# Gated recurrence and max-out MLP in one kernel: first loads in another order, unit 1's steps up to its masks ahead of MoE 0

## The chip, the cores and the metric

The kernel runs on one NeuronCore of a Trainium2 chip. The metric is the device time of one execution in microseconds; lower is better. The core has a matrix engine (TensorE, PE), a vector engine (VectorE, DVE), a scalar engine (ScalarE, ACT), a general engine (GpSimd, POOL) and a queue that here issues all DMAs (SyncE, SP). Each takes its instructions strictly in order, and they wait for each other through semaphores.

## The reference, cut to what matters

```python
batch, n_heads, seq, head_dim = (4, 8, 768, 48)      # q, k, v, alpha
for t in range(S):
    state = alpha[:, :, t, :, None] * state + np.einsum('bhd,bhe->bhde', k[:, :, t], v[:, :, t])
    y[:, :, t] = np.einsum('bhd,bhde->bhe', q[:, :, t], state)
x = y.transpose(0, 2, 1, 3).reshape(B * S, H * D)     # 3072 x 384
h1 = x @ w1                                           # w1, w2: 384 x 1024
h2 = x @ w2
out = np.maximum(h1, h2) @ w_out                      # w_out: 1024 x 384
```

A gated linear recurrence over 768 steps, then an MLP with a max of two branches. Everything comes and goes in float32.

## The kernel before, in words

The recurrence is done in chunks of 128 steps. A **unit** is two chunks of one batch entry with all 8 heads (256 tokens); there are 12 units, u = 0 to 11, and unit u continues the state of unit u - 4. For a unit the attention part is, in this order: ln (ScalarE: logarithm of alpha), sums (TensorE: running sums of it), exps (ScalarE: expm, expp for both chunks, then expd), kmul (GpSimd) and qmul (VectorE), which scale k and q, turn (TensorE transposes, copied by VectorE into qk), vcast (GpSimd and ScalarE: v to 16 bit), pmm and pmask (TensorE products of q and k; VectorE masks them into pt), kvmm, kvsum and state (the chunk's contribution to the state; state makes sb on GpSimd), ystate and yin (TensorE: the outputs y, copied to xn by ScalarE), xturn (transposes y to xt).

The MLP of a unit ("MoE u") is four steps hid (TensorE, then a relu that makes gT) and two steps outp. The max is rewritten: max(h1, h2) = relu(h1 - h2) + h2. So hid uses w12 = w1 - w2 (wsub, VectorE, one quarter of the columns at a time), and h2 @ w_out becomes x @ w2o with w2o = w2 @ w_out. That product is made in the kernel once: w2h is w2 in 16 bit, wturn transposes it into w2T, wcast makes w_out 16 bit (half by ScalarE, half by GpSimd), wmul multiplies into three accumulators wq, wout copies them to w2o.

All steps are written out by hand and every engine gets its instructions in the order of the program text (`tc.manual_schedule()`, L465). So a step that stands earlier in the text stands earlier in the queue of each engine it uses, SyncE's too. The loads of units 0 and 1 and of the weights stand first (L113 to L122); load(2) to load(5) stand in the hand-written start, load(u + 4) at the head of iteration u of the loop from L569. Loads rotate through four buffers (ldp). The loop runs attention of unit u beside the MLP of unit u - 1 and prepares unit u + 1; iteration u begins with kvmm(u, 0).

Two places matter for what follows. The result tile of a unit has two buffers, and both copies of a unit come before its one DMA to memory, which SyncE issues in its order (after load(u + 5)):

```python
X["outs"] = mp.tile([128, 2, DM], FP32, tag="outs", bufs=2, name="outs")   # L412
nc.scalar.copy(out=X["outs"][:, n, :], in_=op)                             # L420
nc.sync.dma_start(out=dst, in_=X["outs"])                                  # L426
```

And the accumulator banks are shared by tags: "m" (two banks) serves hid, outp, wturn and the warm-up matmuls (dummies, which keep TensorE busy and have no use for the result), "pp" (two) serves pmm, "g" (four) the rest of the attention part.

Of the kernel before, what the change touches and what calls it, by code (L numbers as in the profile page):

```python
# [15 lines left out]
def kernel(  # L16
# [73 lines left out]
    def load_a(u):  # L90
        load_fat(u, "af", alpha)
# [8 lines left out]
    def load(u):  # L100
        load_a(u)
        if u in PAIRED:
            load_fat(u, "kf", k)
            load_fat(u, "qf", q)
        else:
            load_kq(u, 0)
            load_kq(u, 1)
        load_v(u)
# [4 lines left out]
    load(0)  # L113
    for ds in range(ND):
        nc.sync.dma_start(out=w2f[:, ds], in_=moe_w2[ds * 128 : (ds + 1) * 128])
    for n in range(2):
        f = slice(n * NF // 2, (n + 1) * NF // 2)
        nc.sync.dma_start(out=wof[:, f], in_=moe_w_out.rearrange("(s p) d -> p s d", p=128)[:, f])
    for n in range(4):
        f = slice(n * DFF // 4, (n + 1) * DFF // 4)  # L120
        nc.sync.dma_start(out=w1f[:, :, f], in_=moe_w1.rearrange("(s p) f -> p s f", p=128)[:, :, f])  # L121
    load(1)  # L122

    wz = constp.tile([128, 512], FP16)
    nc.vector.memset(wz, 0.0)
# [57 lines left out]
    def new(tag, shape, dtype, bufs, name):  # L183
        return psp.tile(shape, dtype, tag=tag, bufs=bufs, name=name)


    def ln(u):
        X = st[u]
        X["lg"] = LG[u % NB]
        nc.scalar.activation(  # L190
            out=X["lg"][:, :, :, 0:D], in_=X["af"].rearrange("p h j d -> p j h d"), func=ACTF.Ln
        )
# [15 lines left out]
    def sums(u):  # L208
        X = st[u]
        lg = X["lg"]  # L210
        cs = [new("g", [128, 512], FP32, 4, "cs") for _ in range(2)]
        X["csv"] = csv = [x[:, 0 : H * D].rearrange("p (h d) -> p h d", h=H) for x in cs]
        X["dps"] = dps = cs[0][:, H * D : H * D + 4 * HP].rearrange("p (j b n) -> p j b n", j=HP, b=2)
        for hp in range(HP):
            for j in range(2):
                nc.tensor.matmul(
                    dps[:, hp], lhsT=pair(lg[:, j], hp), rhs=halves, start=(j == 0), stop=(j == 1)
                )
        for j in range(2):
            for i in range(2):  # L220
                if u in PAIRED:
                    m, x = mf[:, j, i].rearrange("p c t -> p (c t)"), lg[:, j, :, 0:D]
                else:
                    r = slice(64 * i, 64 * i + 64)
                    m, x = mc[r, j], lg[r, j, :, 0:D]
                nc.tensor.matmul(csv[i], lhsT=m, rhs=x, start=(j == 0), stop=(j == 1))  # L226
        X["qn"], X["kn"], X["Em"] = [], [], []
        for cc in range(2):
            X["qn"].append(QN[(2 * u + cc) % (2 * NB)])
            X["kn"].append(KN[(2 * u + cc) % (2 * NB)])  # L230

    def expm(u, cc):
        X = st[u]
        Em = gp.tile([128, H, D], FP32, tag="Em", name="Em")
        X["Em"].append(Em)
        nc.scalar.activation(out=Em, in_=X["csv"][cc], func=ACTF.Exp, scale=-1.0)  # L236

    def expp(u, cc):

        X = st[u]  # L240
        nc.scalar.activation(out=X["csv"][cc], in_=X["csv"][cc], func=ACTF.Exp)  # L241
# [106 lines left out]
    def ystate(u):  # L348
        X = st[u]
        X["ya"] = ya = [new("g", [128, 2, HP, D], FP32, 4, "ya") for _ in range(2)]  # L350
        X["begun"] = begun = set()
        for cc in range(2):
            if ("sb", cc) not in X:
                continue
            for j in range(HP):
                for a in range(2):
                    r = slice(64 * a, 64 * a + D)
                    nc.tensor.matmul(
                        ya[a][:, cc, j, :], lhsT=X["qk"][r, cc, j, :], rhs=X["sb", cc][r, j, :],
                        start=a not in begun, stop=False,  # L360
                    )
                    begun.add(a)

    def yin(u):
        X = st[u]
        ya, begun = X["ya"], X["begun"]
        for cc in range(2):
            for a in range(2):
                for j in range(HP):
                    nc.tensor.matmul(  # L370
                        ya[a][:, cc, j, :], lhsT=X["pt", cc][:, a, j, :], rhs=X["v16"][:, cc, 2 * j + a, :],
                        start=a not in begun, stop=(cc == 1 and j == HP - 1),
                    )
                    begun.add(a)
        X["xn"] = xn = gp.tile([128, 2, HP, 2, D], FP16, tag="xn", name="xn")
        for a in range(2):
            nc.scalar.copy(out=xn[:, :, :, a, :], in_=ya[a])  # L377

    def xturn(u):
        X = st[u]  # L380
        xp = new("g", [128, ND, 2, C], FP16, 4, "xp")
        for cc in range(2):
            xf = X["xn"][:, cc].rearrange("p j a d -> p (j a d)")
            for ds in range(ND):
                o = xp[:, ds].rearrange("p j (c t) -> p c j t", c=2)[:, cc]
                nc.tensor.transpose(o, xf[:, ds * 128 : (ds + 1) * 128], ident)  # L386
        X["xt"] = mp.tile([128, ND, 2, C], FP16, tag="xt", bufs=3, name="xt")
        nc.vector.tensor_copy(out=X["xt"], in_=xp)  # L388

    def hid(u, f2, on_act=None):  # L390
        X = st[u]
        if f2 == 0:
            X["gT"] = mp.tile([128, NF, 2 * C], FP16, tag="gT", name="gT")
        gT = X["gT"]
        hp = new("m", [128, 2, 2 * C], FP32, 2, "hp")
        for n in range(2):
            f = 2 * f2 + n
            for ds in range(ND):
                nc.tensor.matmul(  # L399
                    hp[:, n, :], lhsT=w12[:, ds, f * 128 : (f + 1) * 128],  # L400
                    rhs=X["xt"][:, ds].rearrange("p n t -> p (n t)"), start=(ds == 0), stop=(ds == ND - 1),
                )
        if f2 != 3 if on_act is None else on_act:
            nc.scalar.activation(out=gT[:, 2 * f2 : 2 * f2 + 2, :], in_=hp, func=ACTF.Relu)  # L404
        else:
            nc.vector.tensor_relu(out=gT[:, 2 * f2 : 2 * f2 + 2, :], in_=hp)  # L406
# [21 lines left out]
    def wturn(ds):  # L428
        wt = new("m", [128, NF, 128], FP16, 2, "wt")
        for f in range(NF):  # L430
            nc.tensor.transpose(wt[:, f, :], w2h[:, ds, f * 128 : (f + 1) * 128], ident)
        nc.vector.tensor_copy(out=w2T[:, :, ds * 128 : (ds + 1) * 128], in_=wt)

    wqs = []

    def wmul(n):

        if n == 0:
            wqs.extend([new("pp", [128, DM], FP32, 2, "wq") for _ in range(2)] + [new("g", [128, DM], FP32, 4, "wq")])
        for ds in range(ND):  # L440
            for f in range(4 * n, 4 * n + 4):
                nc.tensor.matmul(  # L442
                    wqs[ds], lhsT=w2T[:, f, ds * 128 : (ds + 1) * 128], rhs=wo16[:, f, :],
                    start=(f == 0), stop=(f == NF - 1),
                )
# [5 lines left out]
    def wcast(n):  # L451
        nc.scalar.copy(out=wo16[:, 4 * n : 4 * n + 2], in_=wof[:, 4 * n : 4 * n + 2])
        nc.gpsimd.tensor_copy(out=wo16[:, 4 * n + 2 : 4 * n + 4], in_=wof[:, 4 * n + 2 : 4 * n + 4])

    def wsub(n):
        f = slice(n * DFF // 4, (n + 1) * DFF // 4)
        nc.vector.tensor_sub(out=w12[:, :, f], in0=w1f[:, :, f], in1=w2f[:, :, f])

    def dummies(n):

        warm = new("m", [128, 512], FP32, 2, "warm")
        for _ in range(n):
            nc.tensor.matmul(warm, lhsT=wz[:, 0:128], rhs=wz, start=True, stop=True)  # L463
# [29 lines left out]
    pmm(0, 1)  # L493
    pmask(0, 1)
    kvsum(0, 1)
    ystate(0)
    dummies(2)
    wturn(1)
    yin(0)
    wturn(2)  # L500
    wcast(0)
    dummies(2)
    xturn(0)
    ln(1)
    dummies(4)
    wmul(0)
    wcast(1)
    wsub(0)
    wsub(1)
    wsub(2)  # L510
    wsub(3)
    wmul(1)
    sums(1)
    wout()

    load(3)
    hid(0, 0, False)
    expm(1, 0)
    expp(1, 0)
    hid(0, 1, True)  # L520
    kmul(1, 0)
    qmul(1, 0)
    expm(1, 1)
    expp(1, 1)
    hid(0, 2, False)
    expd(1)
    kmul(1, 1)
    qmul(1, 1)
    vcast(1)
    hid(0, 3, True)  # L530
    load(4)
    turn(1, 0)
    turn(1, 1)
    outp(0, 0)
    kvmm(1, 0)
    pmm(1, 0)
    kvmm(1, 1)
    kvsum(1, 0)
    state(1, 1)
    pmask(1, 0)  # L540
    kvsum(1, 1)
    ln(2)
    dummies(3)
    pmm(1, 1)
    pmask(1, 1)
    ystate(1)
    outp(0, 1)
    yin(1)
    sums(2)
    exps(2)  # L550
    dummies(3)
    xturn(1)
    for cc in range(2):
        kmul(2, cc)
    state(2, 0)
    vcast(2)
    for cc in range(2):
        qmul(2, cc)
    dummies(2)
    hid(1, 0)  # L560
    hid(1, 1)
    turn(2, 0)
# [84 lines left out]
```

## Time and profile before

| what | value |
|---|---|
| median of 7 runs | 156.89 us (156.48 to 157.63) |
| the profiled execution | 156.89 us, span 155.2 us |
| mean granted TensorE clock | 0.978 |
| TensorE busy | 140.3 us, 90% |
| VectorE, ScalarE, GpSimd busy | 93.9, 91.5, 56.4 us |
| moved by DMA | 28.58 MB, mean 184 GB/s |
| share of the end's chain on TensorE | 68% |

The span runs from the first to the last instruction. All times given as moments are counted from its start. In the lists of a profile a line gives the start, the duration, the engine, the line of the kernel, the operation with out<-in and shapes, how many were merged (x), and in brackets how long the engine stood idle before and what ended that. A busy TensorE need not be at its peak: matmuls are pipelined, and the granted clock says how fast it may run.

### The profile page before, as it was taken

The page shows a single profiled execution, that of the slowest core. Times are in us where ns is not written, and L with a number is a line of the kernel's source. Part 1 is how long each engine was busy: PE and PEld are TensorE (multiplying, and loading weights), DVE is VectorE, ACT ScalarE, POOL GpSimd, SP SyncE. Part 2 cuts the span into 40 slices and gives each one's busy share as a digit, 9 for nine tenths or more (in the row PEclk, how much of TensorE's full clock was granted, in tenths as well). Part 3 has the DMA queues.
Part 4 walks back from the last instruction along what each step waited for, and adds up shares of the span by engine and source line. Part 5 has one row for each costly group of instructions (what it writes and reads, how often), then busy time and mean ns, then how long its engine had stood idle before and what let it go on. Part 6 is the DMA issues. An engine that isn't in the chain of part 4 may idle for free.

```text
span 155.2 us, 4245 instructions
## 1 busy us (share of the span) xinstructions
PE 140.3 (90%) x1683; PEld 101.3 (65%) x1683; DVE 93.9 (60%) x191; ACT 91.5 (59%) x188; POOL 56.4 (36%) x111
## 2 busy tenths in 40 slices
PE   6956982999999898999999999999999999999991
PEld 2334741575677586777787777877778778767760
DVE  5068682075548878776687784957757577664110
ACT  3565404483293778576696584966938669444421
POOL 7481300065071626319046172371632806410000
PEclk9999598699999999999999999999999999999999
DMA  4999999989797999969989799997989002020202
GB/s 115 265 384 376 359 299 224 207 154 246 132 252 121 275 200 200 183 123 315 160 250 194 138 298 143 257 188 148 300 135 301 8 6 95 4 101 4 94 7 101
DMA packets 76339, 28.58 MB, mean 184 GB/s; under 512 B 71712, under 2 KB 74528, under 8 KB 76320
## 3 DMA queue, kind: packets, MB, share of 16 engines
q1 hardware_dynamic: 76320, 28.32, 79.3%
q8 instruction: 13, 0.21, 0.6%
q14 instruction: 6, 0.05, 0.1%
HBM read 23.59 MB, written 4.72 MB: 182 GB/s over the span
## 4 chain that ended last, share of the span: by engine, by line
PE 68%; SPq 8%; DMA 7%; DVE 6%; ACT 5%; issue 4%; POOL 1%; ACTq 0%; DVEq 0%
PE op L417 20%; PE hp L399 16%; PE op L415 8%; DMA af<-in_alpha_dram 7%; PE tp L285 6%; SPq L121 4%; PE pp L334 3%; PE cs L226 3%; DVE pt L340 3%; PE wq L442 2%; SPq L75 2%; PE xp L386 2%; PE ya L370 2%; PE kv L307 2%; ACT cs L241 2%
## 5 line engine op out<-in xcount | busy, mean ns | idle before, releaser
L274 POOL TENSOR_TENSOR kn<-kf,Em 128x384 f16<-128x384 f32 x24 | 23.5, 998 | 35.3 <-ACT Em L236 33.8
L399 PE MATMUL hp<-xt,w 128*128 128x256 f16 x288 | 35.7, 273 | 0.4 <-DVE xt L388 0.2
L417 PE MATMUL op<-wo,gT 128*128 128x384 f16 x192 | 35.1, 326 | 0.0
L340 DVE TENSOR_TENSOR pt<-pp,um 128x512 f16<-128x512 f32 x48 | 30.9, 686 | 3.1 <-PE pp L334 2.4
L420 ACT COPY outs<-op 128x384 f32<-128x384 f32 x24 | 11.5, 479 | 35.4 <-PE op L417 35.4
L399 PEld LDWEIGHTS <-w 128*128 128x128 f16 x288 | 26.7, 98 | 5.0 <-issue 1.0
L417 PEld LDWEIGHTS <-gT 128*128 128x128 f16 x192 | 18.8, 98 | 12.4
L266 POOL TENSOR_TENSOR sb<-tm,dd 128x192 f16<-128x192 f32 x20 | 10.1, 506 | 42.2 <-DVE tm L320 23.1
L404 ACT ACTIVATE gT<-hp 128x512 f16<-128x512 f32 x35 | 20.8, 598 | 4.8 <-PE hp L399 3.8
L292 DVE COPY qk<-tp 128x1024 f16<-128x1024 f16 x20 | 13.7, 687 | 11.7 <-PE tp L285 11.7
L406 DVE TENSOR_SCALAR gT<-hp 128x512 f16<-128x512 f32 x13 | 9.0, 692 | 16.1 <-PE hp L399 16.1
L320 DVE TENSOR_TENSOR tm<-kv,sb 64x192 f32<-64x192 f32 x32 | 11.3, 352 | 8.7 <-PE kv L307 8.4
L415 PE MATMUL op<-w2o,xt 128*128 128x384 f16 x72 | 15.6, 325 | 0.5
L278 DVE TENSOR_TENSOR qn<-qf,cs 128x384 f16<-128x384 f32 x24 | 12.3, 547 | 5.3 <-ACT de L246 5.0
L190 ACT ACTIVATE lg<-af 128x768 f16<-128x768 f32 x12 | 10.1, 843 | 8.1 <-DMA af<-in_alpha_dram 7.8
L377 ACT CAST xn<-ya 128x384 f16<-128x384 f32 x24 | 10.4, 491 | 4.8 <-PE ya L370 4.4
L204 ACT CAST v<-vf 64x384 f16<-64x384 f32 x24 | 12.2, 510 | 1.4 <-DMA vf<-in_v_dram 0.9
L463 PE MATMUL warm<-wz 128*128 128x512 f16 x35 | 11.9, 462 | 1.3 <-DVE halves L146 1.3
L236 ACT ACTIVATE Em<-cs 128x384 f32<-128x384 f32 x24 | 11.8, 490 | 1.9 <-PE cs L226 1.4
L202 POOL CAST v<-vf 64x384 f16<-64x384 f32 x24 | 12.0, 501 | 0.8
L334 PE MATMUL pp<-qk 48*128 48x128 f16 x192 | 10.4, 217 | 1.6 <-DVE pt L340 1.2
L241 ACT ACTIVATE cs<-cs 128x384 f32<-128x384 f32 x24 | 11.8, 492 | 0.0
(60 smaller groups left out, 166.9 us busy)
## 6 DMA issues: line engine op xcount, KB each, us to landing
af<-in_alpha_dram SPq DMA_DIRECT2D x12, 384.0 KB, 5.7
vf<-in_v_dram SPq DMA_DIRECT2D x12, 384.0 KB, 4.9
out_dram<-outs SPq DMA_DIRECT2D x11, 384.0 KB, 4.3
kf<-in_k_dram SPq DMA_DIRECT2D x40, 96.0 KB, 4.4
qf<-in_q_dram SPq DMA_DIRECT2D x40, 96.0 KB, 4.0
w2f<-in_moe_w_dram SPq DMA_DIRECT2D x3, 512.0 KB, 5.9
wof<-in_moe_w_out_dram SPq DMA_DIRECT2D x2, 768.0 KB, 9.0
w1f<-in_moe_w_dram SPq DMA_DIRECT2D x4, 384.0 KB, 10.9
```

The costliest lines, as they stand in the source:

```text
L202: nc.gpsimd.tensor_copy(out=o, in_=i)
L204: nc.scalar.copy(out=o, in_=i)
L241: nc.scalar.activation(out=X["csv"][cc], in_=X["csv"][cc], func=ACTF.Exp)
L274: nc.gpsimd.tensor_mul(out=X["kn"][cc][:, :, 0:D], in0=part(u, "kf", cc), in1=X["Em"][cc])
L278: nc.vector.tensor_mul(out=X["qn"][cc][:, :, 0:D], in0=part(u, "qf", cc), in1=X["csv"][cc])
L292: nc.vector.tensor_copy(out=X["qk"][:, cc], in_=tp.rearrange("p n h t -> p (n h) t"))
L334: nc.tensor.matmul(pa[a][:, j, :], lhsT=qk[r, 1, j, :], rhs=qk[r, 0, j, :], start=True, stop=True)
L340: nc.vector.tensor_mul(out=pt[:, a], in0=X["pa", cc][a], in1=um.unsqueeze(1).to_broadcast([128, HP, C]))
L399: nc.tensor.matmul(hp[:, n, :], lhsT=w12[:, ds, f * 128 : (f + 1) * 128], rhs=X["xt"][:, ds].rearrange("p n t -> p (n t)"), start=(ds == 0 ...
L404: nc.scalar.activation(out=gT[:, 2 * f2 : 2 * f2 + 2, :], in_=hp, func=ACTF.Relu)
L415: nc.tensor.matmul(op, lhsT=X["xt"][:, ds, n, :], rhs=w2o[:, ds, :], start=(ds == 0), stop=False)
L417: nc.tensor.matmul(op, lhsT=X["gT"][:, f, n * C : (n + 1) * C], rhs=wo16[:, f, :], start=False, stop=(f == NF - 1))
```

## The change

The three big loads alpha, k and q of unit 1 move from behind all the weights to between w2 and w_out; w1 becomes the last of the weights, and v of unit 1 stays behind it. In the hand-written start the steps of unit 1 from ln to pmask move from beside and behind MoE 0 to ahead of it, and are interleaved with the making of w2o. Two of the three wq accumulators take banks of tag "m" instead of "pp". The four relus of MoE 0 all go to ScalarE. wsub is spread between pmask and the hid steps. Warm-up matmuls are regrouped (33 instead of 35). The loop from L569 and the computation are the same. New line numbers are 3 higher behind the loads.

```diff
     load(0)
     for ds in range(ND):
         nc.sync.dma_start(out=w2f[:, ds], in_=moe_w2[ds * 128 : (ds + 1) * 128])
+    load_a(1)
+    load_fat(1, "kf", k)
+    load_fat(1, "qf", q)
     for n in range(2):
         f = slice(n * NF // 2, (n + 1) * NF // 2)
         nc.sync.dma_start(out=wof[:, f], in_=moe_w_out.rearrange("(s p) d -> p s d", p=128)[:, f])
     for n in range(4):
         f = slice(n * DFF // 4, (n + 1) * DFF // 4)
         nc.sync.dma_start(out=w1f[:, :, f], in_=moe_w1.rearrange("(s p) f -> p s f", p=128)[:, :, f])
-    load(1)
+    load_v(1)
...
         if n == 0:
-            wqs.extend([new("pp", [128, DM], FP32, 2, "wq") for _ in range(2)] + [new("g", [128, DM], FP32, 4, "wq")])
+            wqs.extend([new("m", [128, DM], FP32, 2, "wq") for _ in range(2)] + [new("g", [128, DM], FP32, 4, "wq")])
...
     pmm(0, 1)
     pmask(0, 1)
     kvsum(0, 1)
+    dummies(2)
+    wturn(1)
+    ln(1)
+    dummies(2)
+    sums(1)
     ystate(0)
-    dummies(2)
-    wturn(1)
+    exps(1)
     yin(0)
+    kmul(1, 0)
+    kmul(1, 1)
     wturn(2)
+    dummies(2)
+    qmul(1, 0)
+    qmul(1, 1)
+    xturn(0)
+    turn(1, 0)
+    dummies(2)
+    turn(1, 1)
     wcast(0)
-    dummies(2)
-    xturn(0)
-    ln(1)
-    dummies(4)
+    pmm(1, 0)
+    pmask(1, 0)
     wmul(0)
     wcast(1)
     wsub(0)
+    pmm(1, 1)
+    pmask(1, 1)
+    wmul(1)
+    wout()
+
+    load(3)
+    hid(0, 0, True)
     wsub(1)
+    hid(0, 1, True)
     wsub(2)
+    dummies(2)
+    hid(0, 2, True)
     wsub(3)
-    wmul(1)
-    sums(1)
-    wout()
-
-    load(3)
-    hid(0, 0, False)
-    expm(1, 0)
-    expp(1, 0)
-    hid(0, 1, True)
-    kmul(1, 0)
-    qmul(1, 0)
-    expm(1, 1)
-    expp(1, 1)
-    hid(0, 2, False)
-    expd(1)
-    kmul(1, 1)
-    qmul(1, 1)
+    dummies(2)
     vcast(1)
     hid(0, 3, True)
     load(4)
-    turn(1, 0)
-    turn(1, 1)
     outp(0, 0)
     kvmm(1, 0)
-    pmm(1, 0)
     kvmm(1, 1)
     kvsum(1, 0)
     state(1, 1)
-    pmask(1, 0)
     kvsum(1, 1)
     ln(2)
-    dummies(3)
-    pmm(1, 1)
-    pmask(1, 1)
+    outp(0, 1)
     ystate(1)
-    outp(0, 1)
     yin(1)
     sums(2)
+    dummies(2)
+    xturn(1)
     exps(2)
-    dummies(3)
-    xturn(1)
     for cc in range(2):
         kmul(2, cc)
...
         qmul(2, cc)
-    dummies(2)
     hid(1, 0)
     hid(1, 1)
```

More of the change, by code (lines that the diff above doesn't have):

```diff
@@ L495 @@
     kvsum(0, 1)
-    ystate(0)
     dummies(2)
     wturn(1)
+    ln(1)
+    dummies(2)
+    sums(1)
+    ystate(0)
+    exps(1)
     yin(0)
+    kmul(1, 0)
+    kmul(1, 1)
     wturn(2)
+    dummies(2)
[5 more added lines that the diff above has]
+    turn(1, 1)
     wcast(0)
-    dummies(2)
-    xturn(0)
-    ln(1)
-    dummies(4)
+    pmm(1, 0)
+    pmask(1, 0)
     wmul(0)
@@ L508 @@
     wsub(0)
-    wsub(1)
-    wsub(2)
-    wsub(3)
+    pmm(1, 1)
+    pmask(1, 1)
     wmul(1)
-    sums(1)
     wout()
     load(3)
-    hid(0, 0, False)
-    expm(1, 0)
-    expp(1, 0)
+    hid(0, 0, True)
+    wsub(1)
     hid(0, 1, True)
-    kmul(1, 0)
-    qmul(1, 0)
-    expm(1, 1)
-    expp(1, 1)
-    hid(0, 2, False)
-    expd(1)
-    kmul(1, 1)
-    qmul(1, 1)
+    wsub(2)
+    dummies(2)
+    hid(0, 2, True)
+    wsub(3)
+    dummies(2)
     vcast(1)
```

## The prediction

> **What bounds the kernel now.** The page first: it cuts the 155.2 us span into forty slices of 3.88 us.
>
> ```profile
> PE   6956982999999898999999999999999999999991
> PEclk9999598699999999999999999999999999999999
> DMA  4999999989797999969989799997989002020202
> ```
>
> TensorE is full from about 31 us on; its holes and its only low-clock slices lie in the first 30 us, where the change works. But the transfers too are busy until 120 us, and that decides this forecast. The chain of waits, in order of time, says what fills the start:
>
> ```profile
> 13.88 10.66 DMA af<-in_alpha_dram
> 24.55 0.84 ACT lg L190
> 25.40 0.73 ACT wo L452
> 26.17 3.76 PE wq L442 x12
> ```
>
> ScalarE waits for unit 1's alpha, issued behind all weights and landing at 13.88 + 10.66 = 24.5; the second wcast stands behind ln(1) on its queue though its data had landed at 17.1 (issue 7.29 + 9.8), and wmul(1) waits for that. Next, equal stretches with TensorE's granted clock (columns: stretch; busy us of PE, PEld, DVE, ACT, POOL; clock; DMA share; GB/s):
>
> ```profile
> 12.50:15.90 3.40, 1.86 (x40) 1.31 (x38) 3.35 (x8) 1.21 (x2) 1.11 (x2) 1.00 1.06 375
> 15.90:19.30 3.40, 3.40 (x37) 2.67 (x35) 2.01 (x5) 1.59 (x3) 0.99 (x2) 0.50 1.08 356
> 22.70:26.10 3.40, 0.00 (x0) 0.00 (x0) 1.37 (x2) 1.55 (x2) 0.00 (x0) 1.00 0.94 217
> 26.10:29.50 3.40, 3.33 (x11) 1.62 (x11) 0.00 (x0) 0.97 (x3) 0.00 (x0) 0.51 1.06 248
> ```
>
> A stretch of 3.4 us that is empty, or only 55% busy (1.86 of 3.40), is followed by 3.4 us at half clock: the same twelve wq matmuls took 2.11 us at 20.50 and 3.76 at 26.17, so one such stretch costs up to 1.65 us.
>
> Last, the place that I expect to matter afterwards: the output of unit 1 on SyncE, then ScalarE and TensorE in iteration u = 4 (start, duration).
>
> ```profile
> 67.51 0.52 SPq L426 DMA_DIRECT2D out_dram<-outs  x1
> ```
> ```profile
> out_dram<-outs SPq DMA_DIRECT2D x1, 384.0 KB, 5.2
> ```
> ```profile
> 73.72 0.48 ACT L420 COPY outs<-op 128x384 f32<-128x384 f32 x1 [1.08 <-PE op L417]
> 74.23 1.04 ACT L204 CAST v<-vf 64x384 f16<-64x384 f32 x2
> ```
> ```profile
> 75.24 1.46 PE L417 MATMUL op<-wo,gT 128*128 128x384 f16 x8
> 76.54 0.33 PE L307 MATMUL kv<-v,kn 128*128 128x96 f16 x4
> ```
>
> The tile outs has two buffers, so the copy at 73.72 (unit 3) may not start before the output of unit 1 has landed, at 67.51 + 5.2 = 72.7. It had 1.0 us to spare. That output was ready at 55.4; it went out at 67.5 because SyncE issues in order and had loads 5 and 6 before it.
>
> **The start, part by part.** Up to pmm(0,1) at 13.9 nothing changes. *Loads.* The third part of w2 lands at 6.4 + 6.5 = 12.9 as before. Loads of 384 KB land 1.3 to 1.5 apart (25.9, 27.4, 28.7 for unit 1), so alpha, k, q of unit 1 land at 14.4, 15.8, 17.3 instead of 24.5, 25.9, 27.4. The halves of w_out (2.1 apart before) then land at 19.4 and 21.5 instead of 15.0 and 17.1; w1's quarters (6.0 for four) at 23.0, 24.5, 26.0, 27.5 instead of 19.6 to 23.1; v of unit 1 at 28.7, as before: the bytes ahead of it are the same. On SyncE's queue three issues (1.3 to 1.5 each when not blocked) pass ahead of six weight issues; the engines hold 4 to 6 us of issued work all the time, which covers that.
>
> *Unit 1 ahead of MoE 0.* ScalarE: ln(1) 14.4 to 15.2. TensorE: dummies and wturn(1) to 15.4, sums(1) (1.0) to 16.4, ystate(0), yin(0), wturn(2), dummies to 18.4 (0.3, 0.55, 0.6, 0.45), all at full clock, since the hole 13.9 to 15.35 is now filled. ScalarE: exps(1) take 1.75 (6.40 to 8.15 for unit 0), so xn(0), queued behind them, ends at 19.05 (before 18.5): xturn(0) is 0.4 later, of no account. VectorE: qmuls to 19.8, xt, two qk copies (0.7 each) to 21.8; GpSimd: kmuls 17.0 to 19.0, wcast 20.3. TensorE: turns to 21.0, pmm(1,0) 22.3, wmul(0) (2.1) 24.4, pmm(1,1) 24.8, wmul(1) 26.9. VectorE alternates pmask(1,0) to 23.5, wsub(0) 25.0, pmask(1,1) 26.3 and the other wsubs (0.95 each) to 29.1, each after its quarter of w1. Since wq now sits in the m banks, hid(0,0) also waits for wout's first copy (26.0): hidden. hid(0,0) starts at 26.9; before, 30.6.
>
> *From there to hid(1,0).* Before 13.7 (30.62 to 44.34). After: four hid (0.75) with four dummies 3.9, two outp 3.6, kvmm 0.6, ystate and yin 0.85, sums(2) 0.75, dummies 0.45, xturn and its copy 1.15: 11.3. The turns, the pmm behind pmask and four of eight dummies left this stretch. The relus moved from VectorE (0.69) to ScalarE (0.60) hide behind the hids; vcast(1) (v at 28.7) is done at 31.4, needed at 32.6. Thus hid(1,0) is at 38.2 instead of 44.3: **6.1 us earlier**. If w1 is 1 us late, wsub(3) has 0.9 to spare; if the clock drops once, 1.65 goes; I keep 4 to 6.5.
>
> **What is late next.** Loads of the later units keep pace with a shift of 6: the tightest, v of unit 3, lands at 45.2 and is needed at 53.8 - 6 = 47.8. The outputs do not. Every wait that SyncE has on an engine up to 67.5 is satisfied long before (load 6's buffers are free from 46 us), the DMA share of its stretches from 30 to 66 averages 1.0, so SyncE's stream is set by the transfers alone and doesn't get faster when TensorE does. The output of unit 1 still lands at about 72.7, while the outs copy of unit 3 would be due at 73.7 - 6.1 = 67.6. ScalarE stands for 5 us. Queued behind it: vcast(5), outs(3,1), ln(6), then gT. TensorE can end outp(3,1) at 70.6, then kvmm(5,0) needs v's first cast: 72.7 + 0.48 + 0.04 + 0.51 + 0.06 = 73.8. Before it started at 76.5, so **2.7 us of the 6.1 remain**, and TensorE stood for 3.2 us. The next output (77.24 + 4.8 = 82.0) meets a copy due at 83.8 - 2.7 = 81.1: 0.9 late, but kvmm has 1.6 to spare there. After that the spare grows.
>
> **The clock.** A hole of 3.2 us in stretches of 3.4 leaves one of them less busy than the 55% of the row above, so I expect half clock after it: bounds 0 and 1.65. Part of the low stretch can fall in the wait itself; I take 1.3, near the row. Net 2.7 - 1.3 = 1.4. The Trainium skill (TensorE: Matmul & The Clock Gate, Part 1) states that the clock falls after at least one idle window of about 3.4 us; by that rule a 3.2 us hole is spared and the time would be 154.2. The row at 12.5, throttled after a hole of only 1.5 us within it, speaks against that, and here the row decides.
>
> **Sum.** The profiled execution took 156.89 (span 155.2 and 1.69 around it), equal to the median 156.89: 156.9 - 1.4 = **155.5 us**.
>
> **Rivals.** (1) *The wait without the clock*: full clock through the hole; 156.9 - 2.7 = 154.2. For: the phase of the stretches is not the program's. Against: both rows above. (2) *The start's gain kept*: outputs leave earlier, nothing waits; 156.9 - 6.1 = 150.8. Against: SyncE's order and a full DMA row. (3) *Slower: the stream of loads starts later.* Before, kf and qf of unit 1 blocked SyncE for 4.62 and 2.69 us against 1.33 for vf, up to 4.7 too long, and the DMA share fell to 0.55 at 25.2 to 26.0. If the same blocking now stands ahead of w_out and w1 and the engines run dry, all later loads and the output of unit 1 slip by d; kvmm(5,0) is at 73.8 + d plus 1.3 for the clock, so it is slower once d passes 1.4; at d = 2.5 158.0. Against: the same bytes, and 4 to 6 us of issued work as cover. (4) *The start gains nearly nothing*, because w_out and w1 come 4.4 us later and hold wmul and hid(0,0): 156.5 to 157.2. Against: wmul(1) is at 24.8 by its TensorE queue, w_out at 21.5.
>
> **How the numbers follow.** Half a per cent, 0.8 us, is about what a measurement of this kernel can tell from no change. Main case 50% (154.9 to 156.3; 0.44 of it faster, 0.06 same); rival 1 17%; rival 2 7%; rival 3 16% (0.13 slower, 0.03 same); rival 4 10% (0.08 same, 0.02 slower). Faster 0.68, same 0.17, slower 0.15. The range, 153.8 to 157.4, leaves out rival 2 and the larger half of rival 3.
>
> **What would show it.** Right: lg of unit 1 near 14.4; no empty stretch at 22.7; hid(1,0) near 38; the output of unit 1 issued at 67 to 68; an idle time of ScalarE of 4 to 5 us before outs(3,0), ended by that DMA; a TensorE hole near 71 to 74, a low clock after it, and from there a lead of 1 to 3 us that stays. Wrong: that output issued well before 66 or after 69, or the lead gone before iteration u = 2.

## The result, and the profile after

The changed kernel took 158.24 us (median of 14 runs, 157.64 to 159.07) against 156.79 (35 runs) on the same chip: ratio 1.0079, 95% interval 1.0054 to 1.0103. It is slower by 0.8%, where 0.9% faster was forecast. (Three of the ten executions of one later run, the one with TensorE kept busy, fell into a slower state, and its ratio leaves them out.) Its profiled execution took 158.15 us, span 156.4. Lines of the changed kernel are three higher from load_v on: the copy into outs is L423, the output DMA L429.

The same three rows of its page (slices of 3.91 us):

```profile
PE   6859879998789899991699999999999999999991
PEclk9999999999999999998579999999999999999998
DMA  4999999879799998979989799898998402020202
```

The low clock of the first 30 us is gone; one empty slice (the digit 1, at 70 to 74 us) and one low-clock stretch behind it are new. The start did what was forecast. Timeline, ScalarE's lg of unit 1 and TensorE's hid(0,0) and hid(1,0) (start, duration, and in brackets the idle time before and what ended it):

```profile
14.49 0.84 ACT L193 ACTIVATE lg<-af 128x768 f16<-128x768 f32 x1 [0.46 <-DMA af<-in_alpha_dram]
```
```profile
26.15 1.67 PE L402 MATMUL hp<-xt,w 128*128 128x256 f16 x12
37.58 1.47 PE L402 MATMUL hp<-xt,w 128*128 128x256 f16 x12 [0.65 <-DVE xt L391]
```

The stretches that were shown of before, in the same view and then the hole, in the steps of 3.41 us in which the clock changed:

```profile
12.50:15.90 3.40, 3.27 (x52) 2.12 (x50) 3.36 (x7) 2.06 (x3) 0.51 (x1) 1.00 1.27 267
15.90:19.30 3.40, 2.73 (x46) 1.75 (x44) 2.75 (x7) 2.51 (x7) 1.96 (x2) 1.00 1.11 344
22.70:26.10 3.40, 3.40 (x28) 1.93 (x27) 2.68 (x5) 1.72 (x3) 0.83 (x1) 1.00 1.12 335
26.10:29.50 3.40, 3.32 (x24) 2.07 (x22) 2.57 (x3) 2.09 (x5) 0.52 (x2) 1.00 1.13 222
```
```profile
70.06:73.47 3.41, 0.83 (x6) 0.29 (x3) 0.05 (x1) 0.00 (x0) 0.00 (x0) 1.00 0.82 240
73.47:76.88 3.41, 1.02 (x13) 0.68 (x14) 0.40 (x2) 2.01 (x5) 0.00 (x0) 0.50 1.14 221
76.88:80.30 3.42, 3.42 (x28) 2.45 (x28) 2.21 (x5) 1.67 (x3) 0.51 (x1) 0.50 0.73 132
```

The first stretch of the hole has 0.83 us of TensorE work, the second 1.02; two stretches, not one, run at half clock, the second and the one behind it. The chain of waits names the cause:

```profile
69.47 5.25 DMA out_dram<-outs
74.71 0.02 issue
74.73 0.02 ACTq L423
74.75 0.04 issue
74.79 0.48 ACT outs L423
75.27 0.02 issue
75.29 0.52 ACT v L207
75.81 0.04 issue
75.86 0.50 PE kv L310 x4
```

The output of unit 1 goes out at 69.47, not 67.51, and lands at 74.7, not 72.7. The copy outs(3,0) waits for it with 8 us of ScalarE idle in front, v of unit 5 is cast behind that copy, and TensorE stands until 75.86. From the timeline of TensorE, kvmm(5,0), the hid behind it, and kvmm(6,0); then, of the kernel before, hid(1,0) and kvmm(6,0):

```profile
75.86 0.50 PE L310 MATMUL kv<-v,kn 128*128 128x96 f16 x4 [4.97 <-ACT v L207]
77.13 2.76 PE L402 MATMUL hp<-xt,w 128*128 128x256 f16 x12
87.82 0.33 PE L310 MATMUL kv<-v,kn 128*128 128x96 f16 x4
```
```profile
44.34 1.47 PE L399 MATMUL hp<-xt,w 128*128 128x256 f16 x12 [0.22 <-DVE xt L388]
86.59 0.33 PE L307 MATMUL kv<-v,kn 128*128 128x96 f16 x4
```

Of a lead of 6.76 us at hid(1,0) (44.34 to 37.58), 0.68 is left at kvmm(5,0) (76.54 to 75.86). From there to kvmm(6,0) it takes 11.96; before it took 10.05 (76.54 to 86.59). The 1.91 us between are the half clock: twelve hid matmuls in 2.76 instead of 1.47. Thus 156.89 - 0.68 + 1.91 = 158.12, against 158.15 measured.

### The profile page after: what moved, and what is told of

The parts are those of the page before. It is cut to its first block, busy times and chain, and to the rows that moved or that the text cites. A ratio compares the mean times of both kernels' runs of the same rounds, so it can differ in the third digit from the quotient of the medians.

```text
span 156.4 us, 4240 instructions
## 1 busy us (share of the span) xinstructions
PE 139.5 (89%) x1681; PEld 99.7 (64%) x1681; DVE 92.4 (59%) x189; ACT 92.7 (59%) x190; POOL 56.5 (36%) x111
## 4 chain that ended last, share of the span: by engine, by line
PE 54%; SPq 22%; DMA 7%; ACT 6%; DVE 4%; issue 4%; ACTq 0%; DVEq 0%
PE op L420 17%; PE hp L402 13%; SPq L75 9%; SPq L85 7%; PE op L418 7%; PE tp L288 5%; DMA vf<-in_v_dram 4%; DMA out_dram<-outs 3%; PE pp L337 3%; SPq L124 3%; PE cs L229 2%; DVE pt L343 2%; PE kv L310 2%; ACT cs L244 2%; PE xp L389 2%
## 5 line engine op out<-in xcount | busy, mean ns | idle before, releaser
L402 PE MATMUL hp<-xt,w 128*128 128x256 f16 x288 | 37.4, 279 | 1.6 <-ACT gT L407 0.8
L423 ACT COPY outs<-op 128x384 f32<-128x384 f32 x24 | 11.5, 479 | 38.0 <-PE op L420 30.1
L402 PEld LDWEIGHTS <-w 128*128 128x128 f16 x288 | 27.2, 100 | 7.5 <-issue 2.6
L407 ACT ACTIVATE gT<-hp 128x512 f16<-128x512 f32 x37 | 22.0, 598 | 6.9 <-PE hp L402 6.0
L409 DVE TENSOR_SCALAR gT<-hp 128x512 f16<-128x512 f32 x11 | 7.6, 692 | 8.0 <-PE hp L402 8.0
L466 PE MATMUL warm<-wz 128*128 128x512 f16 x33 | 11.0, 449 | 1.3 <-DVE halves L149 1.3
```

Source lines behind the costliest of these rows:

```text
L402: nc.tensor.matmul(hp[:, n, :], lhsT=w12[:, ds, f * 128 : (f + 1) * 128], rhs=X["xt"][:, ds].rearrange("p n t -> p (n t)"), start=(ds == 0 ...
```

## The experiments

Theory 1: the start's gain is eaten by the wait of outs(3,0) for the output of unit 1, which lands later than before, and by the clock behind the hole. Rivals: the gain is lost to later loads, or to another queue. Landings below are the issue's start plus the time to landing; "lead" is against the kernel before.

**A third buffer of outs, in the changed kernel and in the kernel before.**

```diff
-X["outs"] = mp.tile([128, 2, DM], FP32, tag="outs", bufs=2, name="outs")
+X["outs"] = mp.tile([128, 2, DM], FP32, tag="outs", bufs=3, name="outs")
```

> The changed kernel with three buffers for the result tile instead of two, nothing else. Theory 1 (the lead of 6.8 us at hid(1,0) is lost at one place, where the copy of unit 3's result waits for the output of unit 1, and by the low clock after it): the copy of unit 3 needs no buffer that is still going out, the copy of unit 4 (due at 83.8 - 6.8 = 77) needs the output of unit 1 (landed at 74.7), so no wait; the hole at 71 to 76 and the low clock are gone; 150 to 151 us. Theory 2 (the slipped stream of loads itself is the bound, the output is only the first to show it): the wait turns up at a load, vf or kf of unit 5 or 6, and the time stays at 156 to 158 us.

> The kernel before with three buffers for the result tile. Control for the first run: theory 1 has the copy of unit 3 with 1.0 us to spare in the kernel before, so a third buffer gives nothing: 156.5 to 157.1. If the kernel before also waited for its outputs somewhere, it would be faster by over 0.8 us.

Measured: the changed kernel 150.26 us (ratio to before 0.9572, 0.9517 to 0.9627); the kernel before 156.47 (0.9966, 0.9909 to 1.0024, no difference that can be told). ScalarE's copies outs(3,0) and outs(4,0) of the first:

```profile
67.07 0.48 ACT L423 COPY outs<-op 128x384 f32<-128x384 f32 x1 [1.08 <-PE op L420]
77.12 0.48 ACT L423 COPY outs<-op 128x384 f32<-128x384 f32 x1 [1.08 <-PE op L420]
```

Both wait for TensorE alone. The output of unit 1 landed at 74.0 here, almost as late, and it did not matter. kvmm(5,0) stood 6.65 us ahead (76.54 to 69.89):

```profile
69.89 0.33 PE L310 MATMUL kv<-v,kn 128*128 128x96 f16 x4
```

The start's gain arrives whole, and 156.89 - 6.65 = 150.24. The wait, not the loads, held it, and the same buffer is worth nothing where nothing waits.

**The output ahead of load 6, two buffers.** In the changed kernel load(u+4) moves to the end of iteration u.

```diff
-        if u + 4 < NU:
-            load(u + 4)
...
+        if u + 4 < NU:
+            load(u + 4)
```

> The changed kernel with load(u+4) moved from the start to the end of iteration u, so that SyncE issues the output of unit 1 behind load 5 and before load 6; outs keeps its two buffers. Theory 1 (the wait is made by SyncE's order, the output queued behind a load that is not urgent): the output of unit 1 lands some 5 us earlier, at 68 to 70, when the copy outs(3,0) is due at about 67.5; the wait shrinks to 0 to 2 us, no low clock follows, 150 to 152. Theory 2 (the transfers themselves are the limit: what goes out first delays the loads behind it by as much): v or k of unit 5 or 6 comes late instead, and the time stays above 155.

Measured: 150.55 us (0.9613, 0.9551 to 0.9675). SyncE's issue of the output of unit 1, and outs(3,0):

```profile
60.12 0.52 SPq L429 DMA_DIRECT2D out_dram<-outs  x1
```
```profile
67.10 0.48 ACT L423 COPY outs<-op 128x384 f32<-128x384 f32 x1 [1.08 <-PE op L420]
```

Theory 1 again, by the other end: the output leaves 9.4 us earlier (69.47 to 60.12), lands at 65.4 (earlier than the 68 to 70 expected), and two buffers are enough. The loads behind it were not late enough to be felt.

**TensorE kept busy in the wait.**

```diff
+if u == 5:
+    warm = new("pp", [128, 512], FP32, 2, "warm")
+    for _ in range(23):
+        nc.tensor.matmul(warm, lhsT=wz[:, 0:128], rhs=wz, start=True, stop=True)
     kvmm(u, 0)
```

> The changed kernel with 23 matmuls on a zero tile (128 x 512 each, about 5 us at full clock) put on TensorE's queue just before kvmm(5,0): TensorE is busy in the wait for the copy outs(3,0), and the wait itself is unchanged (the output of unit 1 should still land near 74.7, kvmm(5,0) start at 75.9 to 76.2). Theory 1 (the loss after the wait is the half clock that follows the empty stretch, 1.96 us between kv(5,0) and kv(6,0)): no 0.50 in 74 to 80, kv(6,0) near 85.9 instead of 87.82, time 156.2 to 156.7, about the kernel before. Theory 2 (the loss after it comes from something else, as ScalarE's queue or v of unit 5 coming late): the clock is high and the time stays at 157.6 to 158.6.

Measured: ratio to before 0.9991 (0.9953 to 1.0029), where the changed kernel has 1.0079; the profiled execution took 156.05. TensorE in the wait and after it:

```profile
70.20 5.13 PE L576 MATMUL warm<-wz 128*128 128x512 f16 x23
75.70 0.34 PE L310 MATMUL kv<-v,kn 128*128 128x96 f16 x4 [0.37 <-ACT v L207]
85.75 0.33 PE L310 MATMUL kv<-v,kn 128*128 128x96 f16 x4
```

kvmm(5,0) stands where it stood (75.70 against 75.86), and kvmm(6,0) follows after 10.05, the time of before, at full clock. So the 1.91 us are the clock's, and without them the change would be worth nothing, not a loss. How much the filling brings is less sure than that: the ratios differ by 0.9%, 1.4 us, the two profiled executions by 2.1, and 156.05 is the shortest of the executions in the ratio (up to 157.73, median 156.88, above the 156.2 to 156.7 expected).

**The parts alone.** First the new order of loads with the steps of before, with two and with three buffers of outs.

```diff
+    load_a(1)
+    load_fat(1, "kf", k)
+    load_fat(1, "qf", q)
...
-    load(1)
+    load_v(1)
```

> The kernel before with only the loads in the new order; the steps stand as before. What it tells apart is why the output of unit 1 lands at 74.7 instead of 72.7. Theory A (the order of the first loads: SyncE is blocked later, at af and kf of unit 2, and the engines run partly dry at 28 to 34 us): the slip is there too, out of unit 1 lands at 74 or later, and as the start still gains some 2 to 4 us (ln(1) no longer holds the second wcast) that copy waits again: 156.5 to 158.5. Theory B (the earlier steps slow the transfers or delay their issue): the output lands at 72.7 plus or minus 0.4, and the time is 155 to 156.5.

> The new order of the first loads alone (steps of the kernel before), with three buffers of outs instead of two. Theory 1 (the new order of the loads moves hid(1,0) 3.45 us ahead, and of that the wait on the output of unit 1 took 2.0 again): no TensorE hole before kv(5,0), 152.7 to 153.7. Theory 2 (the later landing of the loads, not of the output, eats the lead): as with two buffers, 155.3 to 156.4. With both parts of the change and three buffers 150.26 was measured; the difference to this run is what the moved steps are worth once nothing waits.

Measured: 155.89 (0.9925, 0.9864 to 0.9987) and 153.73 (0.9791, 0.9749 to 0.9832). With two buffers, outs(3,0) and kvmm(5,0), and the clock's stretches about them:

```profile
74.05 0.48 ACT L423 COPY outs<-op 128x384 f32<-128x384 f32 x1 [4.86 <-DMA out_dram<-outs]
```
```profile
75.12 0.34 PE L310 MATMUL kv<-v,kn 128*128 128x96 f16 x4 [1.86 <-ACT v L207]
```
```profile
70.98:74.39 3.41, 2.27 (x20) 1.30 (x17) 1.50 (x3) 0.34 (x1) 0.00 (x0) 1.00 1.16 334
74.39:77.81 3.42, 2.69 (x40) 2.25 (x42) 2.20 (x5) 3.29 (x7) 0.51 (x1) 1.00 0.83 119
```

A smaller lead (3.45 at hid(1,0)) meets the same landing, 74.0; the hole is 1.86 us, its stretches hold 2.27 and 2.69 us of work, and the clock stays at 1.00. The kernel with less gain at the start ends 2.3 us ahead of the one with more: kvmm(5,0) stands 0.74 us earlier, and most of the rest is the clock loss that it does not have. Theory A of that run had the landing right (74 or later) and the time too long (156.5 to 158.5). With three buffers the lead arrives: 153.73, and what the moved steps add where nothing waits is 153.73 - 150.26 = 3.5 us (the two were timed on different chips; by their ratios to before it is 2.2%, 3.4 us).

Then the steps and banks of the change with the old order of loads, and the banks alone (tag "m" for "pp" in wmul).

> The changed kernel with its loads in the order of before: the steps of unit 1 stand ahead of MoE 0 but alpha of unit 1 lands at 24.5 again. Both theories: sums(1) waits from 15.4 to 25.4 with all of MoE 0 behind it, so hid(1,0) at 46 to 49 and 159 to 163 us. Theory A: output of unit 1 lands at 72.7 or a little later (the loads' order is that of before); theory B, if it is the steps: 74 or later.

> The kernel before with only the two wq accumulators moved from the tag pp to the tag m; loads and steps as before. Theory 1 (this part is worth nothing, since hid(0,0) waits for w1 and not for the bank): 156.3 to 157.2. Theory 2 (hid(0,0) has to wait for the wo copies that empty the bank): slower by 0.5 to 1.5, 157.5 to 158.5.

Measured: the steps alone 161.66 (one execution), the banks alone ratio 0.9998 (0.9964 to 1.0032). With the steps alone, ScalarE's lg(1), now ahead of unit 0's MoE but with its alpha still last:

```profile
24.21 0.84 ACT L190 ACTIVATE lg<-af 128x768 f16<-128x768 f32 x1 [10.46 <-DMA af<-in_alpha_dram]
```

Everything queued behind it waits too, TensorE 10.05 us in one hole, and the clock was half from 17.6 to 31.2. hid(1,0) comes 4.6 us later than before. The banks cost and bring nothing.

**Why the output lands later.** Four profiles with the old order of loads have it at 72.7 (before), 72.3 (third buffer), 72.4 (steps alone) and 72.1 (banks alone); those with the new order at 74.7 (changed), 74.0 (third buffer), 74.0 and 75.1 (loads alone, two and three buffers) and 74.5 (TensorE kept busy). Four more runs asked what makes it: matmuls that take the lead back, v of unit 2 ahead of its k and q, and two other choices of what goes ahead of the weights.

```diff
 # loads alone, TensorE delayed before hid(0,0)
+    dummies(19)
     hid(0, 0, False)
```

> The new order of the first loads alone, with 19 matmuls on a zero tile (some 4.1 us) ahead of hid(0,0), so that the steps from there on stand about where they stood in the kernel before. It asks why the output of unit 1 lands at 74.0 to 74.7 with the new order of loads and at 72.3 to 72.7 with the old. Theory A (the order of the first loads itself makes the stream later): it lands at 73.6 or later here as well. Theory B (earlier steps do, by their traffic or buffers): it lands at 72.3 to 72.9. Time near the kernel before's, 156 to 158.

```diff
 # the changed kernel, in load(u)
+            if u == 2:
+                load_v(u)
             load_kq(u, 0)
             load_kq(u, 1)
-        load_v(u)
+        if u != 2:
+            load_v(u)
```

> The changed kernel with v of unit 2 issued ahead of the eight k and q loads of unit 2 instead of behind them; all else as changed. It asks why the output of unit 1 lands 1.4 to 2.3 later with the new order of loads (74.0 to 75.1 in six looks against 72.3 to 72.7 in three with the old order). Theory A (by 28 the transfers have caught up with what SyncE has issued: more bytes are moved, 7.7 against 7.5 to 7.7 MB, and then the eight loads of 96 KB, which take 0.65 us of SyncE each, 147 GB/s at most, leave the transfers partly idle, DMA share 0.72 at 28:32 against 0.88 to 1.16; 384 KB more in front would bridge that): the share at 28:32 is 0.9 or more, v of unit 2 lands before 36, the output of unit 1 lands at 72 to 73.5, time 156 to 157.3. Theory B (the stream's lateness is not made there): it lands at 74.0 to 75.1 as before, time 157.6 to 158.6.

```diff
 # the kernel before, only alpha of unit 1 ahead of w_out and w1
+    load_a(1)
...
-    load(1)
+    load_fat(1, "kf", k)
+    load_fat(1, "qf", q)
+    load_v(1)
```

> The kernel before with only the alpha of unit 1 issued between w2 and w_out; k, q and v of unit 1 stay behind w1, steps as before. It asks which of the three early loads makes the stream late and which brings the lead. Theory A (k and q make it late, since they are what blocks SyncE for 4.9 us ahead of the weights): alpha lands at 14.4, the hole at 22.7 goes, hid(1,0) is 2 to 3.5 earlier than 44.3, the output of unit 1 lands at 72.3 to 73.0 as with the old order, kv(5,0) at 73.5 to 74.3, 154.0 to 155.0. Theory B (any load ahead of the weights does): it lands at 74.0 or later, and the time is 155.3 to 156.5, as with all three loads moved.

```diff
 # the kernel before, all of unit 1 ahead of w_out and w1
+    load(1)
...
-    load(1)
```

> The kernel before with all four loads of unit 1 (v too) between w2 and w_out, so that w1 is the last of the first loads; steps as before. Theory A (the transfers run partly dry after the first loads because big loads are used up early and only loads of 96 KB follow): with w1 last the same happens: share at 28:32 about 0.7 to 0.8, the output of unit 1 at 74.0 to 75.1. Theory B (it is the place of v of unit 1 just ahead of unit 2's loads that matters): it lands at 72.3 to 73.0. Time 155.5 to 157.5, since w1 comes 1.3 us later for hid(0,0).

Measured: TensorE delayed, 158.30 (one execution; steps 1.4 us later than before, so the delay was more than the lead), landing 75.0. v of unit 2 first, 157.86 (1.0074, 1.0040 to 1.0108), landing 74.8. Alpha alone, 159.01 (1.0122, 1.0058 to 1.0186), landing 76.1. All of unit 1, 157.60 (one execution), landing 76.1, later than either theory of that run had. So it is the order of the first loads and not the pace of TensorE: with TensorE behind the kernel before, the landing was late all the same. It is not k and q either: with alpha alone the landing is later still, as theory B of that run had it (74.0 or later), but the time is far above the 155.3 to 156.5 that it expected. From the run with alpha alone, TensorE's hid(1,0), 5.0 us ahead, SyncE's output of unit 1, and kvmm(5,0), 0.7 behind:

```profile
39.31 1.47 PE L402 MATMUL hp<-xt,w 128*128 128x256 f16 x12 [0.22 <-DVE xt L391]
```
```profile
70.89 0.52 SPq L429 DMA_DIRECT2D out_dram<-outs  x1
```
```profile
77.20 0.50 PE L310 MATMUL kv<-v,kn 128*128 128x96 f16 x4 [5.53 <-ACT v L207]
```

Theory A of the run with v of unit 2 first (the transfers run partly dry at 28 us) falls as the whole cause. Its equal stretch, the changed kernel's, and that of before:

```profile
28.00:32.00 4.00, 3.89 (x27) 2.38 (x25) 0.90 (x2) 2.70 (x5) 2.21 (x5) 1.00 0.89 187
```
```profile
28.00:32.00 4.00, 3.89 (x27) 2.33 (x24) 0.67 (x1) 2.56 (x5) 2.21 (x5) 1.00 0.72 129
```
```profile
28.00:32.00 4.00, 4.00 (x31) 2.62 (x30) 0.53 (x1) 1.95 (x5) 0.78 (x1) 0.80 1.16 192
```

The transfers moved 187 GB/s there instead of 129, nearly the 192 of before, v of unit 2 landed at 32.3 instead of 38.7, and the output of unit 1 still landed at 74.8: here the stream is slow one stretch later (32 to 36 us: 143 GB/s, before 204). Where it falls behind differs from run to run. The changed kernel has lost its ground by 36 us (9.35 MB moved, before 9.60), and from there to 68 us it moves 193 GB/s against 194. With alpha alone the stream is level until 44 us (11.10 MB, before 11.08) and loses behind that (177 GB/s from 44 to 68 us, before 196). So what in the order of the first loads makes the output land 1.3 to 3.4 us later stays open. One observation of the trace's records bears on it, and was not tested: when SyncE began to issue the second q of unit 2 (at 28.65 us, before 28.57), 1221 packets of data were issued and not yet moved in the changed kernel, 1749 before, and yet that issue took SyncE 1.42 us instead of 0.68. It was held up longer while less was queued; one of the 16 engines full and others nearly empty would fit that, but this is a guess. The Trainium skill (DMA: Bandwidth & Descriptors, Queues, rings and completion order) states that each engine has a ring of its own for a queue; no run here shows a single ring.

## Why the prediction was wrong, by its own steps

- **The start: right.** hid(1,0) was forecast at 38.2 and came at 37.58; lg(1) at 14.4 and 14.49; hid(0,0) at 26.9 and 26.15. The banks were rightly costed at nothing. But the load named as the tightest, v of unit 3, was not: v of unit 2 landed at 38.7 (before 36.6) and held ScalarE for 0.83 us, and the lead fell from 6.76 at hid(1,0) to 5.82 at kvmm(2,0) (42.07, before 47.89). The later wait hid that loss. In the profile with a third buffer of outs v of unit 2 landed at 37.3, and the lead stayed at 6.65.
- **What is late next: the right wait.** outs(3,0) on the output of unit 1, and kvmm(5,0) 1.1 us after the landing (forecast 72.7 and 73.8; measured 74.7 and 75.86). Rival 2 (nothing waits, 150.8) is what the third buffer gives, 150.26.
- **The landing: the step that failed.** "The output of unit 1 still lands at about 72.7" rested on "SyncE's stream is set by the transfers alone and doesn't get faster when TensorE does". It does not get faster, but the new order made it slower, by 2.0 us. The argument against rival 3, "the same bytes, and 4 to 6 us of issued work as cover", held only up to 28 us (8.20 MB moved, before 8.02); from there to 32 the DMA share is 0.72 where it was 1.16, and at 36 us the stream is behind. Why is open, as said above. The forecast's own sign of being wrong, that output issued after 69, is what came (69.47). The order of the first loads was costed by when they land themselves, and not by how the stream behind them runs.
- **The clock: mis-sized.** Taken at 1.3 with a bound of 1.65 for one stretch; it was 1.91. With the hole at 4.97 instead of 3.2 us two stretches held little work, and two ran at half clock; part of the first lay in the wait. The reading that a stretch of 3.4 us only 55% busy is followed by half clock is not general (last section). Rival 1 (no clock loss) holds for the smaller hole of the loads alone, 1.86 us.
- **Sum.** 155.5 + 2.06 (kvmm(5,0) at 75.86 for 73.8) + 0.61 (1.91 for 1.3) = 158.2; measured 158.15. Either error alone leaves the sign no better than open: with the landing as forecast and the same clock loss, 156.89 - 2.7 + 1.9 = 156.1; with no clock loss, 156.2, near the run with TensorE kept busy (156.05 in the profile, median 156.88). Rival 3's outcome is what happened, with d = 2.0 against its deciding point of 1.4, and it had been given 16%; its reason is not: the first loads did not start the stream later, for by 28 us more had been moved than before.
- **After that: right.** The next output was said to be late by 0.9 and hidden. In the run with TensorE kept busy, outs(4,0) waited 1.6 us and kvmm(6,0) did not move.

## What to carry to other kernels

Once work moves ahead into a wait on a fixed landing, the end is set by that landing and no longer by the lead; the lead only lengthens the hole (3.45 us with the loads alone, landing 0.7 us earlier, ended 2.3 us ahead of 6.76 with the whole change). So the landing's own shift by the change has to be bounded on both sides, and where TensorE is the bound, the clock loss behind the hole belongs in the sum with as many stretches as the hole can empty. A result tile with two buffers, whose output queues behind prefetches that are not urgent, deserves a third buffer or an earlier place in the queue before any work at the start: here each turned +0.8% into -4%.

## What the runs showed of the hardware that was not expected

- Half clock also follows stretches of 3.41 us that are not empty: after 0.83, 1.02 and, in the profile before, 1.86 us of TensorE work the next stretch was at 0.50; after 2.27 and 2.69 it stayed at 1.00. But the work in a stretch does not decide it alone. In the run with all of unit 1 ahead, 1.51 us of work were followed by full clock, and only the next stretch, with 1.27, by half:

```profile
17.70:21.11 3.41, 1.51 (x12) 0.74 (x11) 1.03 (x2) 0.09 (x1) 0.00 (x0) 1.00 1.09 354
21.11:24.52 3.41, 1.27 (x8) 0.78 (x8) 0.00 (x0) 1.58 (x3) 0.82 (x1) 1.00 1.08 358
24.52:27.94 3.42, 3.42 (x13) 1.67 (x11) 1.95 (x3) 1.30 (x2) 0.83 (x1) 0.50 1.15 326
```

  So these runs give no limit in us of work. The Trainium skill (TensorE: Matmul & The Clock Gate, Part 1) speaks of an idle window of about 3.4 us; the stretch of before with 1.86 us of work was not idle and was followed by half clock all the same.
- The order of the first loads, with the same bytes, shifted the landing of a transfer issued some 40 us after the last of them had landed by 1.3 to 3.4 us against the profile before, whatever the engines did in between (72.1 to 72.7 in four profiles, 74.0 to 76.1 in nine).
